# Early weight chunks and a diagonal-matrix mix for the first batch of a linear-attention, channel-mix and expert-attention kernel

## The chip, the cores and the metric

The kernel runs on one core of one Trainium2 chip. The metric is the device time of one execution in microseconds (us). A profile shows one execution; its span begins and ends a little inside that execution's own time.

## What is computed

Eight batches of 576 positions go through three blocks. The change touches the first two of them. The reference, cut to these:

```python
kv = np.einsum('bhsd,bhse->bhde', k, v)          # 8 heads of 64
out = np.einsum('bhsd,bhde->bhse', q, kv)
rms = np.sqrt(np.mean(out * out, axis=-1, keepdims=True) + 1e-06)
x = out / rms * g_norm                           # 512 columns in all
x_prev = x shifted by one position, zeros first
xk = mu_k * x + (1.0 - mu_k) * x_prev
xr = mu_r * x + (1.0 - mu_r) * x_prev
kk = np.maximum(xk @ w_k, 0.0)                   # w_k 512 x 1024
vv = kk * kk @ w_v                               # w_v 1024 x 512
x2 = vv / (1.0 + np.exp(-(xr @ w_r)))            # w_r 512 x 512
```

The weights w_r, w_k and w_v are given as float64. The third block, attention of four experts with a gate, reads x2 and stays as it is.

## The kernel before

**Shapes and loops.** Positions lie along the free axis, in two halves of 288 for each batch; features lie along the 128 partitions, in four slices. Each product of the second block is made as three single-pass products of a high and a low part (`mm3`, L60 to L64: wh times xh, wh times xl, wl times xh). `phase1` does the first two blocks batch by batch; `phase2` does the third.

**Weight conversion.** w_r, w_k and w_v are 20 chunks of 128 x 512 float64 numbers, 512 KB each: chunks 0 to 3 are w_r, 4 to 11 w_k, 12 to 19 w_v. `wload` (L134 to L138) asks for a chunk on ScalarE's queue, into one of three buffers `raw`. `wconv` (L167 to L191), at its call number i, finishes chunk i-1, asks for chunk i+2 and starts chunk i: ScalarE writes the magnitudes of the high words to `cvt` (L190), one of three buffers; the generator `words` (L140 to L158) then issues five VectorE steps (L146, L148, L150, L155, L157) and one ScalarE copy (L152); finally the low part is made by a full-precision product and two single-pass ones (L183 to L185) and a ScalarE copy (L186). Chunks 13, 15, 17 and 19 use two VectorE operations (L179, L180) instead of products. `wstep` issues one step of the chunk in work; it is called between the steps of a root.

**The front of a batch.** The generator `front(b)` multiplies keys with values of five position chunks (L229), asks for the next batch's first three key and value chunks, copies the sum to `kv` (L233), and then for each half: multiplies q (L251, `heads`), squares and copies (L256, L257), forms the means with products (L269), takes the reciprocal root on VectorE in 14 dependent steps (`rsqrt`, L276 to L291), spreads it with products (L299) and scales xT (L302). For batch 0 the halves go one after the other.

**The mix.** `mix(b, h, which)` makes the high and the low part of xr or xk of a half, slice by slice: ScalarE scales the shifted column block (L354), VectorE adds the scaled current one (L355), ScalarE rounds to the high part (L356), and the low part is a VectorE subtraction (L348), or, for xr of batch 0, a full-precision product with the identity, a single-pass product with its negative (L344, L345) and a ScalarE copy (L346). `acc`, the PSUM tile of all these products, has four buffers.

**Order.** First all loads are asked for (L415 to L427): weight chunks 0 to 2 on ScalarE's queue, keys, values and q of batch 0 on SyncE's, then the second batch's last two key and value chunks (L423, into tiles that are free until the first k product), and the small vectors. Then the front of batch 0 runs in seven steps with conversions between them as the list `TK` says (L453 to L457); then the xr mix of the first half with four more conversions; then the r products of the first half (L464) with the second batch's front and the second half's xr mix between them; then those of the second half with the first half's xk mix; then the main loop, with k products (L494), v products (L505) and, among the v products of the first half, the second half's xk mix (L508). This written order is not the order on the engines: the framework's scheduler orders each engine's instructions when the program is built, and sets one of a later line ahead of an earlier one where its own timeline has the engine free.

Of the kernel before, what the change touches and what calls it, by code (L numbers as in the profile page):

```python
# [8 lines left out]
F32 = mybir.dt.float32  # L9
F32R = mybir.dt.float32r  # L10
BF16 = mybir.dt.bfloat16
I32 = mybir.dt.int32
U32 = mybir.dt.uint32
AF = mybir.ActivationFunctionType
# [10 lines left out]
def tile_kernel(ctx: ExitStack, tc: tile.TileContext, qT, k, v, g2, mu_k, mu_r, w_r, w_k, w_v, w_qk, w_vg, w_o, out):  # L25
    nc = tc.nc
    P = 128
    B, S, DM = k.shape
# [3 lines left out]
    HS = S // 2  # L32
    KD = DM // P
# [9 lines left out]
    NF = len(FH)  # L43
# [5 lines left out]
    ident = const.tile([P, P], F32, name="ident")  # L49
    g_sb = const.tile([P, 1], F32, name="g_sb")  # L50
    muk = const.tile([P, KD], F32, name="muk")
    mur = const.tile([P, KD], F32, name="mur")
    nuk = const.tile([P, KD], F32, name="nuk")
    nur = const.tile([P, KD], F32, name="nur")
# [52 lines left out]
    def phase1():  # L107
        with ExitStack() as st1:
            w1 = st1.enter_context(tc.tile_pool(name="w1", bufs=1))
            sb = st1.enter_context(tc.tile_pool(name="sb1", bufs=2))  # L110
            ps = st1.enter_context(tc.tile_pool(name="ps1", bufs=1, space=PSUM))
# [13 lines left out]
            stg = stg_.enter_context(tc.tile_pool(name="stg", bufs=2, side="right"))  # L125
            CW = 512
# [3 lines left out]
            raws, cvs, ops = {}, {}, []  # L130

            VEC = (13, 15, 17, 19)

            def wload(i):  # L134
                if i < len(wts):
                    _, _, w, kt, c0 = wts[i]
                    raw = raws[i] = stg.tile([P, CW, 2], I32, name="raw", bufs=3)
                    nc.scalar.dma_start(raw.rearrange("p n t -> p (n t)"), w[kt * P:(kt + 1) * P, c0:c0 + CW].bitcast(I32))  # L138

            def words(i):  # L140
# [26 lines left out]
            def wconv():  # L167

                i = wat[0]
                wat[0] += 1  # L170
                if 0 < i <= len(wts):
                    for _ in ops.pop():
                        pass
                    wh, wl, _, kt, c0 = wts[i - 1]
                    x = cvs.pop(i - 1)
                    raws.pop(i - 1)
                    h, l = wh[:, kt, c0:c0 + CW], wl[:, kt, c0:c0 + CW]
                    if i - 1 in VEC:
                        nc.vector.tensor_sub(x, x, h.bitcast(F32))  # L179
                        nc.vector.tensor_add(l, x, l.bitcast(F32))  # L180
                    else:
                        acc = ps.tile([P, CW], F32, name="acc", bufs=4)
                        nc.tensor.matmul(acc, ident, x, start=True, stop=False)  # L183
                        nc.tensor.matmul(acc, idn, h, start=False, stop=False)
                        nc.tensor.matmul(acc, idn, l, start=False, stop=True)  # L185
                        nc.scalar.activation(l, acc, AF.Copy)  # L186
                    wload(i + 2)
                if i < len(wts):
                    t = cvs[i] = stg.tile([P, CW], F32, name="cvt", bufs=3)
                    nc.scalar.activation(t, raws[i][:, :, 1].bitcast(F32), AF.Abs)  # L190
                    ops.append(words(i))  # L191

# [2 lines left out]
            def load_kv(i, kv=None):  # L195
                b, c = divmod(i, NF)
                if b < B and i not in kvt:
                    t0, n = FH[c]
                    if kv is None:
                        kv = [(fr2[0] if c > 2 else fr).tile([P, DM], F32, name=name, bufs=2 if c > 2 else 3) for name in ("kt", "vt")]  # L200
                    kt, vt = kv
                    nc.sync.dma_start(kt[:n], k[b, t0:t0 + n, :])
                    nc.sync.dma_start(vt[:n], v[b, t0:t0 + n, :])
                    kvt[i] = (kt, vt)
# [12 lines left out]
            def front(b):  # L217
# [51 lines left out]
                                nc.tensor.matmul(sm[g:g + 32, :QS], sels[:, i, :], sqs[h, i // 2][:, i % 2, c * QS:(c + 1) * QS],  # L269
                                                 start=(i == 0), stop=(i == NP - 1), skip_group_check=True)  # L270

                def rsqrt(h0, h1):
                    g = slice(64 * h0, 64 * h1)
                    m, r, t, c = ms[g], y[g], nt[g], rb[g]

                    nc.vector.tensor_scalar(m, sm[g, :QS], -0.5, -0.5e-6, op0=ALU.mult, op1=ALU.add)  # L276
                    wstep()
                    nc.vector.tensor_scalar(t.bitcast(I32), m.bitcast(I32), 1, None, op0=ALU.logical_shift_right)
                    wstep()
                    nc.vector.tensor_scalar(r.bitcast(I32), t.bitcast(I32), -1.0, float(0x5F3759DF + 2 ** 30 - 2 ** 22), op0=ALU.mult, op1=ALU.add)  # L280
                    wstep()
                    for _ in range(3):
                        nc.vector.tensor_mul(t, r, r)
                        wstep()
                        nc.vector.tensor_mul(t, t, m)
                        wstep()
                        nc.vector.scalar_tensor_tensor(r, t, 1.5, r, op0=ALU.add, op1=ALU.mult)
                        wstep()

                    nc.vector.tensor_copy(c, r)  # L290
                    nc.vector.scalar_tensor_tensor(c, c.bitcast(F32), lom[g], r, op0=ALU.mult, op1=ALU.add)  # L291
# [12 lines left out]
                if b == 0:  # L304

                    for h in range(2):
                        for a in range(2):
                            heads(h, a)
                            yield
                        means(h)  # L310
                        rsqrt(h, h + 1)
                        yield
                        scaled(h)
                        yield
                    return
# [12 lines left out]
                    yield  # L328
                    yield

            mixed = {}

            def mix(b, h, which):
                mu, nu = (mur, nur) if which == "r" else (muk, nuk)
                xT = xTs[b]
                xh = sb.tile([P, KD, HS], F32R, name="xh", bufs=2)
                xl = sb.tile([P, KD, HS], F32R, name="xl", bufs=2)
                mixed[b, h, which] = (xh, xl)

                def low(p):  # L340
                    if b == 0 and which == "r":

                        acc = ps.tile([P, 512], F32, name="acc", bufs=4)
                        nc.tensor.matmul(acc[:, :HS], ident, xp, start=True, stop=False)  # L344
                        nc.tensor.matmul(acc[:, :HS], idn, xh[:, p, :], start=False, stop=True)  # L345
                        nc.scalar.activation(xl[:, p, :], acc[:, :HS], AF.Copy)  # L346
                    else:
                        nc.vector.tensor_sub(xl[:, p, :], xp, xh[:, p, :].bitcast(F32))  # L348

                for p in range(KD):  # L350
                    cur = xT[:, p, 1 + h * HS:1 + (h + 1) * HS]
                    prv = xT[:, p, h * HS:(h + 1) * HS]
                    x = sb.tile([P, HS], F32, name="xm", bufs=3)
                    nc.scalar.activation(x, prv, AF.Copy, scale=nu[:, p:p + 1])  # L354
                    nc.vector.scalar_tensor_tensor(x, cur, mu[:, p:p + 1], x, op0=ALU.mult, op1=ALU.add)  # L355
                    nc.scalar.activation(xh[:, p, :], x, AF.Copy)  # L356
                    if p > 0:
                        low(p - 1)
                    xp = x
                    yield  # L360
                low(KD - 1)
                yield
# [42 lines left out]
            def run(*gens):  # L405
                for g in gens:
                    if g is not None:
                        next(g, None)
# [3 lines left out]

            sk2 = [sb.tile([P, KF, HS], F32, name=name, bufs=1).rearrange("p k t -> p (k t)") for name in ("kh", "kl")]
            sq_ = sb.tile([P, KD, HS], F32, name="sg", bufs=2)
            for c in "w0 w1 w2 k0 k1 k2 k3 k4 q0 q1 q2 q3".split():  # L415
                i = int(c[1])
                if c[0] == "w":
                    wload(i)
                elif c[0] == "k":
                    load_kv(i, [sk[:, j * DM:(j + 1) * DM] for j in (2 * i - 6, 2 * i - 5)] if i > 2 else None)  # L420
                else:
                    load_q(i, sq_[:, :2, :] if i > 2 else None)
            for i in (3, 4):  # L423
                load_kv(NF + i, [t[:, (i - 3) * DM:(i - 2) * DM] for t in sk2])
            nc.sync.dma_start(g_sb, g2)
            nc.sync.dma_start(muk, mu_k)
            nc.sync.dma_start(mur, mu_r)  # L427
# [21 lines left out]
            def ticks(n):  # L449
                for _ in range(n):  # L450
                    wconv()

            TK = [1, 0, 1, 1, 0, 1, 1, 1, 1, 1, 1]  # L453
            wconv()
            for i in range(7):
                run(f0)
                ticks(TK[i])  # L457
            mr = mix(0, 0, "r")
            for i in range(4):
                run(mr, f0)  # L460
# [3 lines left out]
            for m in range(KD):  # L464
                r_group(0, 0, m)
                run(f1, mr)
                wconv()
            run(f1, mr)
            mk = mix(0, 0, "k")
            for m in range(KD):  # L470
                r_group(0, 1, m)
# [405 lines left out]
```

## Time and profile before

| | us |
|---|---|
| median of three runs | 1022.28 |
| the three runs | 1023.65, 1022.28, 1021.43 |
| the profiled execution, its own time | 1020.85 |
| its span | 1018.8 |
| TensorE busy in the span | 987.1 |
| VectorE busy | 546.8 |
| ScalarE busy | 500.2 |

In the rows, PE is TensorE's products, PEld its weight loads, DVE is VectorE, ACT ScalarE, POOL GpSimd, SP SyncE; ACTq and SPq are the queues of the latter two, in which transfers are started. L12 is line 12 of the kernel. A row names the tile written and the tiles read, the shape and type of each, and how often. A full-precision product appears as two records. Products are pipelined, and the lengths of neighbouring ones overlap; the distance of their starts tells what one costs.

### The profile page before, as it was taken

Reading aid. Unit: us, or ns where it says so; the run is one execution under the profiler, and the core shown is the slowest. Engines: PE = TensorE matmul, PEld = TensorE weight load, DVE = VectorE, ACT = ScalarE, POOL = GpSimd, SP = SyncE. Lnnn points to the kernel's source line nnn. Section 1 sums busy time; section 2 is a strip of 40 time slices with the busy share of each in tenths; the row PEclk is TensorE's granted clock in tenths of the full one; section 3 lists DMA queues with packets and bytes.
Section 4 is the critical chain, followed back from the end, with each engine's and each line's share of the span. In section 5 each row is a group of like instructions: output and inputs, shape, how many; then the busy total and the mean of one; then the engine's idle time right before and its main releaser. Section 6 shows DMA issues by size and latency. Waiting matters only on the chain.

```text
span 1018.8 us, 21026 instructions
## 1 busy us (share of the span) xinstructions
PE 987.1 (97%) x8168; PEld 899.7 (88%) x8168; DVE 546.8 (54%) x1572; ACT 500.2 (49%) x1326; POOL 248.5 (24%) x408
## 2 busy tenths in 40 slices
PE   6789999999999999999999999999999999999998
PEld 3358999999999999999999999988989898888986
DVE  4889625535535535445355531476575655656552
ACT  4677426434533553463364533456463645464544
POOL 0001212102201210220131113265161625334321
PEclk9789999999999999999999999999999999999999
DMA  9572213041050050050002201211120202020102
GB/s 324 171 231 64 67 60 106 24 112 53 25 151 27 10 164 24 1 165 24 24 2 71 60 5 43 69 48 31 65 71 24 94 1 94 18 77 27 48 12 82
DMA packets 42034, 70.56 MB, mean 69 GB/s; under 512 B 3792, under 2 KB 21712, under 8 KB 41936
## 3 DMA queue, kind: packets, MB, share of 16 engines
q1 hardware_dynamic: 30608, 49.31, 15.4%
q10 hardware_dynamic: 11328, 19.93, 6.3%
q8 instruction: 64, 1.05, 0.5%
q14 instruction: 34, 0.28, 0.1%
HBM read 50.34 MB, written 18.87 MB: 68 GB/s over the span
## 4 chain that ended last, share of the span: by engine, by line
PE 80%; DMA 7%; ACT 4%; POOL 3%; DVE 3%; issue 1%; ACTq 0%; SPq 0%; DVEq 0%; POOLq 0%
PE acc L62 22%; PE acc L64 21%; PE acc L63 21%; PE acc L725 3%; PE pt L698 3%; DMA x2in<-x2d 3%; PE s L649 2%; PE po L251 2%; POOL pr L678 2%; POOL x2l L535 2%; ACT pr L661 2%; PE acc L229 1%; PE acc L269 1%; ACT x2h L534 1%; PE po L299 1%
## 5 line engine op out<-in xcount | busy, mean ns | idle before, releaser
L388 POOL TENSOR_TENSOR ksq<-rl 128x288 f32<-128x288 f32 x128 | 92.8, 727 | 502.8 <-ACT rl L385 475.8
L62 PE MATMUL acc<-xh,wkh 128*128 128x288 f32 x512 | 153.2, 299 | 0.0
L64 PE MATMUL acc<-xh,wkl 128*128 128x288 f32 x512 | 151.6, 296 | 0.0
L64 PE MATMUL acc<-kh,wvl 128*128 128x288 f32 x512 | 151.1, 296 | 0.0
L62 PE MATMUL acc<-kh,wvh 128*128 128x288 f32 x512 | 149.4, 297 | 0.5 <-ACT kh L386 0.4
L63 PE MATMUL acc<-kl,wvh 128*128 128x288 f32 x512 | 149.6, 293 | 0.2 <-DVE kl L389 0.2
L63 PE MATMUL acc<-xl,wkh 128*128 128x288 f32 x512 | 149.4, 292 | 0.0
L661 ACT ACTIVATE pr<-pr,nm 128x256 f32<-128x256 f32 (+4 forms) x144 | 83.2, 580 | 66.5 <-DVE nm L615 65.6
L389 DVE TENSOR_TENSOR kl<-ksq,kh 128x288 fp32r<-128x288 f32 x128 | 64.4, 507 | 72.3 <-POOL ksq L388 70.6
L62 PEld LDWEIGHTS acc<-xh,wkh 128*128 128x128 f32 x512 | 96.2, 188 | 7.1 <-issue 5.3
L678 POOL TENSOR_SCALAR pr<-pr,rc,wg 128x512 f32<-128x512 f32 (+3 forms) x128 | 76.6, 613 | 99.3 <-DVE wg L608 53.9
L63 PEld LDWEIGHTS acc<-kl,wvh 128*128 128x128 f32 x512 | 97.3, 190 | 0.7 <-DVE kl L389 0.4
L63 PEld LDWEIGHTS acc<-xl,wkh 128*128 128x128 f32 x512 | 97.4, 190 | 0.1
L62 PEld LDWEIGHTS acc<-kh,wvh 128*128 128x128 f32 x512 | 95.3, 188 | 1.4 <-ACT kh L386 0.9
L64 PEld LDWEIGHTS acc<-kh,wvl 128*128 128x128 f32 x512 | 96.1, 188 | 0.0
L64 PEld LDWEIGHTS acc<-xh,wkl 128*128 128x128 f32 x512 | 96.0, 188 | 0.0
L374 ACT ACTIVATE sg<-acc 128x288 f32<-128x288 f32 x64 | 25.9, 408 | 142.6 <-PE acc L64 142.6
L348 DVE TENSOR_TENSOR xl<-xm,xh 128x288 fp32r<-128x288 f32 x120 | 54.4, 487 | 75.9 <-ACT xh L356 75.3
L401 DVE TENSOR_TENSOR sg<-acc,sg 128x288 f32<-128x288 f32 x64 | 29.2, 457 | 105.9 <-PE acc L64 105.1
L385 ACT ACTIVATE rl<-acc 128x288 f32<-128x288 f32 x128 | 52.1, 414 | 58.7 <-PE acc L64 58.3
L62 PE MATMUL acc<-x2h,wqh 128*128 128x256 f32 (+1 forms) x256 | 78.6, 308 | 0.0
L62 PE MATMUL acc<-xh,wrh 128*128 128x288 f32 x256 | 77.1, 302 | 1.1 <-ACT wvl L186 1.1
(166 smaller groups left out, 2437.3 us busy)
## 6 DMA issues: line engine op xcount, KB each, us to landing
x2d<-sg SPq DMA_DIRECT2D x16, 576.0 KB, 3.3
qt<-in_qT SPq DMA_DIRECT2D x31, 288.0 KB, 4.8
out<-ob SPq DMA_DIRECT2D x28, 288.0 KB, 2.1
kt<-in_k SPq DMA_DIRECT2D x24, 256.0 KB, 5.2
vt<-in_v SPq DMA_DIRECT2D x24, 256.0 KB, 5.7
x2in<-x2d ACTq DMA_DIRECT2D x8, 640.0 KB, 4.4
raw<-in_w_k ACTq DMA_DIRECT2D x8, 512.0 KB, 4.5
raw<-in_w_v ACTq DMA_DIRECT2D x8, 512.0 KB, 3.5
```

The lines of the kernel that those rows point to most:

```text
L62: nc.tensor.matmul(ps, wh(i), xh(i), start=(i == 0), stop=False)
L63: nc.tensor.matmul(ps, wh(i), xl(i), start=False, stop=False)
L64: nc.tensor.matmul(ps, wl(i), xh(i), start=False, stop=(i == n - 1))
L348: nc.vector.tensor_sub(xl[:, p, :], xp, xh[:, p, :].bitcast(F32))
L385: nc.scalar.activation(rl, acc, AF.Relu)
L388: nc.gpsimd.tensor_mul(sq, rl, rl)
L389: late.append(lambda: nc.vector.tensor_sub(kl[:, m, :], sq, kh[:, m, :].bitcast(F32)))
L401: nc.vector.tensor_mul(sg[:, m, :], acc, sg[:, m, :])
L661: nc.scalar.activation(pr[:, :L], pr[:, :L], AF.Exp, bias=nm, scale=-1.0, accum_out=sms[b, p, j][:, e2:e2 + 1])
L678: nc.gpsimd.tensor_scalar(pr[:, :L], pr[:, :L], rc[:, r:r + 1], wg, op0=ALU.mult, op1=ALU.mult)
L698: nc.tensor.transpose(pt[:, (i - i0) * P:(i - i0 + 1) * P], pr[:, k1 - P:k1], ident)
L725: nc.tensor.matmul(y[r * D:(r + 1) * D, a:w], vs[:, i, e * D:(e + 1) * D], pT[:, r, i, a:w], start=(i == 0), stop=(i == idx[-1]), skip_gro ...
```

## The change

Four edits to `phase1`; all else stays.

- **Loads.** Chunks 3 and 4 are asked for at the start too, into tiles `xh` and `xl` that the mixes use only later. Calls 1 to 3 of `wconv` then ask for chunks 5 to 7, calls 4 and 5 for none, and from call 6 on it is as before. The written order puts chunk 2 behind two pairs of keys and values, chunk 3 before the last pair, chunk 4 behind two q loads. The second batch's last two key and value chunks are asked for after the third step of the front instead of at the start.
- **Order.** `TK` has one more conversion in its second place. In the first root of batch 0 no conversion step is written between its steps.
- **Mix.** For batch 0 a slice is mixed by two full-precision products with diagonal matrices (mu and 1 - mu on the diagonal, made by ScalarE from the identity), the high part is copied out of PSUM, a single-pass product with the negative identity is added, and the low part is copied out. This serves all four mixes of batch 0.
- **Buffers.** `cvt` has two buffers instead of three; the diagonals (`dg`) have one.

```diff
-            def wload(i):
+            def wload(i, raw=None):
...
-                    raw = raws[i] = stg.tile([P, CW, 2], I32, name="raw", bufs=3)
+                    if raw is None:
+                        raw = stg.tile([P, CW, 2], I32, name="raw", bufs=3)
+                    raws[i] = raw
...
-                    wload(i + 2)
+
+                    if i - 1 < 3:
+                        wload(i + 4)
+                    elif i - 1 > 4:
+                        wload(i + 2)
                 if i < len(wts):
-                    t = cvs[i] = stg.tile([P, CW], F32, name="cvt", bufs=3)
+                    t = cvs[i] = stg.tile([P, CW], F32, name="cvt", bufs=2)
...
-                def rsqrt(h0, h1):
+                def rsqrt(h0, h1, wstep=wstep):
...
-                        rsqrt(h, h + 1)
+                        rsqrt(h, h + 1, *([lambda: None] if h == 0 else []))
...
+            def diag(which):
+                dg = dgs[which] = stg.tile([P, 2, KD, P], F32, name="dg", bufs=1)
+                for j, t in enumerate((mur, nur) if which == "r" else (muk, nuk)):
+                    for p in range(KD):
+                        nc.scalar.activation(dg[:, j, p, :], ident, AF.Copy, scale=t[:, p:p + 1])
...
+                if b == 0:
+
+                    dg = dgs[which]
+                    acc = None
+                    for p in range(KD + 1):
+                        if p > 0:
+                            nc.tensor.matmul(acc[:, :HS], idn, xh[:, p - 1, :], start=False, stop=True, skip_group_check=True)
+                            nc.scalar.activation(xl[:, p - 1, :], acc[:, :HS], AF.Copy)
+                        if p < KD:
+                            acc = ps.tile([P, 512], F32, name="acc", bufs=4)
+                            for j in range(2):
+                                nc.tensor.matmul(acc[:, :HS], dg[:, j, p, :], xT[:, p, 1 - j + h * HS:1 - j + (h + 1) * HS], start=(j == 0), stop=(j == 1))
+                            nc.scalar.activation(xh[:, p, :], acc[:, :HS], AF.Copy)
+                        yield
+                    return
...
-            for c in "w0 w1 w2 k0 k1 k2 k3 k4 q0 q1 q2 q3".split():
+            sw = [sb.tile([P, KD, HS], F32R, name=name, bufs=2).rearrange("p k t -> p (k t)")[:, :2 * CW].bitcast(I32).rearrange("p (n t) -> p n t", t=2) for name in ("xh", "xl")]
+            for c in "w0 w1 k0 k1 w2 k2 k3 w3 k4 q0 q1 w4 q2 q3".split():
                 i = int(c[1])
                 if c[0] == "w":
-                    wload(i)
+                    wload(i, sw[i - 3] if i > 2 else None)
...
-            for i in (3, 4):
-                load_kv(NF + i, [t[:, (i - 3) * DM:(i - 2) * DM] for t in sk2])
...
-            TK = [1, 0, 1, 1, 0, 1, 1, 1, 1, 1, 1]
+            TK = [1, 1, 1, 1, 0, 1, 1, 1, 1, 1, 1]
             wconv()
             for i in range(7):
                 run(f0)
+                if i == 2:
+                    for c in (3, 4):
+                        load_kv(NF + c, [t[:, (c - 3) * DM:(c - 2) * DM] for t in sk2])
                 ticks(TK[i])
+                if i == 4:
+                    diag("r")
             mr = mix(0, 0, "r")
...
             run(f1, mr)
+            diag("k")
             mk = mix(0, 0, "k")
```

## Rows read from the trace of the kernel before

**Rows 1.** The page's first part: busy time, share of the span and instructions of each engine.
```profile
PE 987.1 (97%) x8168; PEld 899.7 (88%) x8168; DVE 546.8 (54%) x1572; ACT 500.2 (49%) x1326; POOL 248.5 (24%) x408
```
**Rows 2.** Busy time by stretch: window, length, engines (records), TensorE's clock, transfers' share, GB/s.
```profile
0.00:20.70 20.70, 10.69 (x92) 5.99 (x92) 8.65 (x21) 6.58 (x12) 1.98 (x17) 1.00 0.94 318
20.70:35.20 14.50, 10.13 (x44) 4.43 (x44) 10.62 (x31) 7.27 (x14) 0.00 (x0) 0.76 0.87 289
35.20:68.30 33.10, 27.17 (x203) 16.61 (x203) 27.93 (x65) 24.83 (x51) 0.00 (x0) 0.81 0.57 185
68.30:89.80 21.50, 20.39 (x147) 15.80 (x146) 19.41 (x42) 18.62 (x44) 0.00 (x0) 0.98 0.41 125
89.80:104.10 14.30, 14.30 (x103) 13.64 (x102) 14.30 (x31) 9.45 (x23) 6.29 (x8) 1.00 0.11 39
```
**Rows 3.** Timeline of ScalarE and its queue: start, length, instruction, idle before it.
```profile
19.98 0.34 ACTq L138 DMA_DIRECT2D raw<-in_w_k  x1
20.36 0.38 ACT L233 ACTIVATE kv<-acc 128x256 f32<-128x256 f32 x1 [3.42 <-DMA kl<-in_v]
...
47.59 0.66 ACT L190 ACTIVATE cvt<-raw 128x512 f32<-128x512 f32 x1 [0.27 <-DMA raw<-in_w_k]
...
50.76 0.68 ACT L190 ACTIVATE cvt<-raw 128x512 f32<-128x512 f32 x1 [1.50 <-DMA raw<-in_w_k]
```
**Rows 4.** Timeline of VectorE, first root: first step, its one gap, last step.
```profile
24.77 0.30 DVE L276 TENSOR_SCALAR ms<-acc 64x144 f32<-64x144 f32 x1
...
27.73 0.43 DVE L146 TENSOR_SCALAR cvt<-cvt 128x512 f32<-128x512 f32 x1 [1.11 <-ACT cvt L190]
...
33.62 0.35 DVE L291 SCALAR_TENSOR_TENSOR rb<-rb,lom,y 64x144 fp32r<-64x144 f32 x1
```
**Rows 5.** Timeline of all engines, 36 to 62 us: the landmarks named in the text.
```profile
36.10 1.82 DVE L302 SCALAR_TENSOR_TENSOR xT<-xT,g_sb,po 128x288 f32<-128x288 f32 x4 [2.13 <-issue]
...
44.26 0.31 DVE L276 TENSOR_SCALAR ms<-acc 64x144 f32<-64x144 f32 x1 [1.22 <-PE acc L269]
...
49.47 0.29 PE L62 MATMUL acc<-xh,wrh 128*128 128x288 f32 x1
...
53.76 0.22 PE L229 MATMUL acc<-kl,kh 112*64 112x64 f32 x1
...
54.89 1.12 PE L183 MATMUL acc<-cvt,ident 128*128 128x512 f32 x2
...
60.06 0.67 PE L299 MATMUL po<-rb,selb 32*128 32x144 f32 x8 [1.98 <-DVE rb L291]
```
**Rows 6.** Timeline of TensorE at the full clock.
```profile
75.85 0.65 PE L344 MATMUL acc<-xm,ident 128*128 128x288 f32 x2
...
76.47 1.02 PE L183 MATMUL acc<-cvt,ident 128*128 128x512 f32 x2
...
77.80 0.65 PE L344 MATMUL acc<-xm,ident 128*128 128x288 f32 x2
...
89.88 0.30 PE L62 MATMUL acc<-xh,wkh 128*128 128x288 f32 x1
90.01 0.29 PE L63 MATMUL acc<-xl,wkh 128*128 128x288 f32 x1
```
**Rows 7.** Groups by line and form, first 89.8 us: busy, mean ns, idle before.
```profile
L354 ACT ACTIVATE xm<-xT,nur 128x288 f32<-128x288 f32 x8 | 4.0, 533 | 0.7 <-DVE xT L302 0.7
L355 DVE SCALAR_TENSOR_TENSOR xm<-xT,mur,xm 128x288 f32<-128x288 f32 x8 | 3.9, 513 | 1.0 <-ACT xm L354 1.0
...
L346 ACT ACTIVATE xl<-acc 128x288 fp32r<-128x288 f32 x8 | 3.3, 418 | 0.3 <-issue 0.3
...
L348 DVE TENSOR_TENSOR xl<-xm,xh 128x288 fp32r<-128x288 f32 x4 | 1.7, 450 | 0.0
...
L444 ACT ACTIVATE idn<-ident 128x128 fp32r<-128x128 f32 x1 | 0.3, 309 | 0.0
```
**Rows 8.** Transfers of the first 100 us: issue, KB, us to landing.
```profile
kl<-in_v SPq DMA_DIRECT2D x1, 160.0 KB, 8.0
```

More of the change, by code (lines that the diff above doesn't have):

```diff
@@ L329, in front @@
                     yield
-            mixed = {}
+            mixed, dgs = {}, {}
+            def diag(which):
[3 more added lines that the diff above has]
+                        nc.scalar.activation(dg[:, j, p, :], ident, AF.Copy, scale=t[:, p:p + 1])
             def mix(b, h, which):
@@ L338, in mix @@
                 mixed[b, h, which] = (xh, xl)
-                def low(p):
[L341 to L348, printed above, removed]
+                if b == 0:
[12 more added lines that the diff above has]
+                    return
+                def low(p):
+                    nc.vector.tensor_sub(xl[:, p, :], xp, xh[:, p, :].bitcast(F32))
                 for p in range(KD):
```

## The prediction

> **What bounds the kernel now.** The page's first part comes first: TensorE is busy 97% of the span [rows 1]. The stretches of the first 104 us show where the rest is. I count as lost what a stretch leaves over after TensorE's busy time multiplied by its granted clock: 20.7 - 10.69 x 1.00 = 10.0 us, 14.5 - 10.13 x 0.76 = 6.8, 33.1 - 27.17 x 0.81 = 11.1, 21.5 - 20.39 x 0.98 = 1.5, and nothing in the last: 29.4 us [rows 2]. The first k product starts at 89.88 [rows 6], and from there TensorE is full. So **the end is TensorE's work plus the time it loses before 90 us**; a change pays what it adds to the one and gains what it takes from the other. VectorE is busy 14.30 of 14.3 us in the last stretch and 19.41 of 21.5 before it, but TensorE loses little there: what VectorE is spared after 68 us buys almost nothing [rows 2].
>
> What loses the 29.4 us is read from the order on each engine. The copy of kv, behind which all of the first half stands, ran at 20.36 us, because a weight load sat in ScalarE's queue until 19.98 and waited for a load of values to land; ScalarE idled 3.42 us for it [rows 3]. The first root began at 24.77 and its last step at 33.62, 9.2 us to its end, with ten conversion steps of two chunks (the first at 27.73) and a gap of 1.11 us among its fourteen [rows 4]. From its scaling (36.10) to the first r product (49.47) pass 13.4 us; the second root runs from 44.26 to the product that reads it, 60.06 [rows 5]. Inside it ScalarE waited 1.50 us for a weight chunk [rows 3].
>
> **What the change costs on TensorE.** A full-precision product of 288 columns and its correction took 76.47 - 75.85 = 0.62 us at the full clock, a single-pass product 90.01 - 89.88 = 0.13, so the full one is 0.49 [rows 6]. The mix of one 128-row slice becomes two full products and one correction, 1.11 us; four mixes of four slices are 16 x 1.11 = 17.8 us. Gone are the eight full products and eight corrections of the two r mixes, 8 x 0.62 = 5.0. **TensorE's work grows by 12.8 us**, and by the accounting above all of it is paid; the last mix, 4.4 us, stands among the v products after 104 us, where nothing can cover it.
>
> **What it moves off the other engines.** VectorE loses 16 multiply-adds of 0.51 us and the 8 subtractions of the k mixes of 0.45, 11.8 us [rows 7]. ScalarE loses 16 scalings of 0.53 (8.5 us) and gains 8 copies of the low part of 0.42 (3.3) and 16 diagonals; the nearest row for one is the 128x128 copy of 0.31, so 5.0 [rows 7]. That is even, taken as nothing. The first eight diagonals stand beside the first root, where ScalarE is busy half of the time; the other eight (2.5 us) fall where it is busy 18.62 of 21.5 us, and could be felt if a copy stood behind them [rows 2].
>
> **What it recovers** of the 29.4, stretch by stretch [rows 2]:
> - *To 20.7 us.* Chunks 3 and 4 are asked for early. Chunk 3 can be converted while TensorE waits for keys, 1.3 us of its work (three products from 76.47 to 77.80 [rows 6]). ScalarE's 3.42 us before the kv copy may go, 2.7 of them after the last key product; but chunk 5's load takes the place of chunk 3's in ScalarE's queue: it waits for chunk 0's buffer, and behind it stand the magnitudes of the next chunks and the kv copy. Against it, chunk 3's 512 KB go ahead of the last keys, at 318 GB/s 1.6 us. Ends -1.6 and 4.0; I take 2.5, nearer to the upper end, since the queue wait is the longer of the two.
> - *To 35.2.* The root's own fourteen steps, the first 0.30 and the last 0.35, are by estimate 4.2 us [rows 4] of 9.2. Ends 0 and 5.0. I take 3.5: the gap of 1.11 goes and chunks 3 and 4 lie behind VectorE, but steps of a chunk written later stood inside this root too, so some will again.
> - *To 68.3.* From scaling to the first r product I get 1.8 us of scaling, four slices of two ScalarE copies (4 x 0.84), and one slice's latency of 3.1 at 1.2 GHz (two products of 0.98, two copies, a correction), 8.3 us by estimate from [rows 5 to 7], against 13.4. The second root keeps its interleaving; what goes is the mix among its steps and, as chunks 5 to 7 are asked for two conversions earlier, waits such as the 1.50. Chunk 8 onwards is asked for as before. Ends 0 and 11.1; I take 8.5, the 5.1 just found and some of the second root.
> - *To 89.8.* TensorE is without work 1.1 us. Ends 0 and 1.5; I take 1.2.
>
> Sum: 2.5 + 3.5 + 8.5 + 1.2 = 15.7 recovered, 12.8 paid: **-2.9 us**. The ends, all together, are -8.8 and +14.4.
>
> The Trainium skill (DMA: Bandwidth & Descriptors, Issuing engines are not separate DMA queues) says that transfers started by different engines run on the same 16 engines and interleave, so that another issuing engine saves little more than issue time. By it the early chunks only displace keys, the first term is -1.6, and the sum is +1.2. The transfer engines, 94% busy in the first 20.7 us, support it [rows 2]; the held kv copy is a wait of ScalarE's queue, of which it does not speak.
>
> **Edits with no price.** The loads of the second batch's last keys and values go behind that batch's first three pairs on SyncE's queue. The slowest took 8.0 us to land [rows 8]; their first reader runs at 53.76 [rows 5], and asked for at 27 us they are there by 35: free while that lead of 18 us stands. The q loads behind them start four issues later and serve products after 60 us. The small mu loads move up. One conversion earlier in the written order moves no work off any engine. The mixes hold a PSUM buffer over two ScalarE copies instead of one: between nothing and 16 x 0.42 = 6.7 us, taken as nothing, since four buffers stand in turn and a slice comes only between groups.
>
> **The rivals.** *The roots stay filled (slower).* Ten conversion steps of two chunks stood in the first root although the code writes only one chunk's there [rows 4]; with two more chunks landed there is more to put in. Then the second stretch gives 0, the third 5.0, the first 1.0, the last 0: 6.0 recovered, +6.8, 1029.1. It decides as soon as less than 10.8 is recovered. Against it: it needs the filling to be as dense while VectorE has 11.8 us less to do. The Trainium skill (Perfetto Trace Analysis, Identifying the Most-Contended Engine) points the same way: improve the engine with the highest occupancy first; this change loads it. TensorE's 97% agrees that it is that engine.
> *VectorE paced the front.* If its 11.8 us come through almost whole, all stretches go near their ends: 21 recovered, -8.2, 1014.1. For it: VectorE is busy 27.93 of 33.1 us in the third stretch; against it: 8.65 of 20.7 and 10.62 of 14.5 in the first two [rows 2].
> *The two cancel*, within 2 us: 1022.3.
> *Two conversion buffers pace the chunks (slower).* A chunk held its buffer from its magnitudes (47.59 [rows 3]) to the end of its first product (54.89 and 0.56 [rows 5]), 7.9 us; with two buffers that is a chunk every 3.9 us, where the next one came after 3.2 (50.76). Over the eight chunks of w_v that is 5.6 us, and the first v product waits for the last of them: 1025.
>
> **How the numbers follow.** The profiled execution took 1020.85 us by its own time, 2.05 around its span, and the runs' median is 1022.28, 1.43 above it; -2.9 gives 1017.95 beside the profile and 1019.4 beside the median. Under 0.2%, 2 us, a measurement of this kernel cannot be told from no change. Chances: the forecast (2 to 6 us faster) 0.28, VectorE as pacer 0.20, cancelling 0.20, filled roots 0.24, two buffers 0.08. So faster 0.48, same 0.20, slower 0.32. The likeliest case's own range is 1016 to 1020; cases of both signs hold the chance, so the range goes from 1012, which leaves out the best part of the pacer case, to 1029, which takes in most of the filled roots.
>
> **What would show it.** Right: the kv copy before 20 us; the first root in under 6 us; the first r product before 45; the first k product some 7 us before 89.88, although 8.4 of the added 12.8 us stand ahead of it (all but the last mix); the granted clock near 1.00 from 35 us. Wrong: conversion steps inside the first root as densely as now, a kv copy behind a weight load, magnitudes waiting for a conversion buffer, or a first k product later than 85.5 us, which leaves no room for the last mix.

## The result, and the profile after

The changed kernel takes 1033.95 us, the median of four runs (1033.38 to 1035.8), the kernel before 1021.86 on the same chip: ratio 1.0126 [1.0109, 1.0143]. **It is slower by 12 us**, outside the predicted range. The profiled execution took 1033.38 us, its span 1031.6, 12.8 more than before. Lines of the changed kernel stand up to 20 further down: the weight load is L140, the magnitudes L196, the full-precision product of a conversion L185, the kv copy L239, the diagonals L343, the mix L358 to L364.

The page's first part after [rows 1]:
```profile
PE 997.5 (97%) x8224; PEld 909.9 (88%) x8224; DVE 536.5 (52%) x1548; ACT 501.3 (49%) x1334; POOL 246.2 (24%) x408
```
VectorE is relieved by 10.3 us, ScalarE is even, TensorE has the added work. The same stretches as in [rows 2]:
```profile
0.00:20.70 20.70, 9.37 (x48) 4.78 (x50) 9.42 (x24) 6.39 (x10) 1.87 (x16) 0.92 0.95 329
20.70:35.20 14.50, 11.11 (x94) 6.14 (x90) 9.98 (x26) 12.18 (x26) 0.11 (x1) 0.85 0.92 305
35.20:68.30 33.10, 24.27 (x183) 16.05 (x183) 22.89 (x56) 14.85 (x30) 0.00 (x0) 0.81 0.46 152
68.30:89.80 21.50, 21.50 (x130) 15.35 (x129) 14.41 (x28) 18.66 (x43) 0.00 (x0) 0.99 0.47 153
89.80:104.10 14.30, 14.30 (x111) 12.17 (x110) 12.99 (x32) 8.18 (x18) 0.00 (x0) 1.00 0.12 38
```
By the prediction's formula (length less busy time times granted clock) TensorE loses 12.1, 5.1, 13.4, 0.2 and 0: **30.8 us, where the kernel before lost 29.4** and the forecast left 13.7. Nothing was recovered. The first k product starts at 98.4 (before 89.88), the first v product at 114.0 (104.1).

**The start.** ScalarE and its queue after [rows 3]:
```profile
15.55 0.34 ACTq L140 DMA_DIRECT2D raw<-in_w_k  x1
16.01 0.66 ACT L196 ACTIVATE cvt<-raw 128x512 f32<-128x512 f32 x1 [5.07 <-DMA xT<-in_k]
...
24.49 0.38 ACT L239 ACTIVATE kv<-acc 128x256 f32<-128x256 f32 x1 [0.55 <-PE acc L235]
...
28.30 1.28 ACT L343 ACTIVATE dg<-ident,mur 128x128 f32<-128x128 f32 x4
29.47 1.28 ACT L343 ACTIVATE dg<-ident,nur 128x128 f32<-128x128 f32 x4
30.64 0.65 ACT L262 ACTIVATE sq<-po 128x576 f32<-128x576 f32 x1
```
A weight load (15.55, chunk 5) sat in the queue until keys had landed, by the row that names what ended the wait, and with the magnitudes behind it ScalarE idled for 5.07 us. TensorE's rows show what follows:
```profile
18.37 2.07 PE L185 MATMUL acc<-cvt,ident 128*128 128x512 f32 x2 [3.30 <-DVE cvt L152]
20.38 1.12 PE L235 MATMUL acc<-vt,kt 128*64 128x64 f32 x16
21.43 0.80 PE L186 MATMUL acc<-wrh,idn 128*128 128x512 f32 x1
22.02 0.63 PE L187 MATMUL acc<-wrl,idn 128*128 128x512 f32 x1
22.58 1.86 PE L235 MATMUL acc<-xT 112*64 112x64 f32 x32
```
The late magnitudes make the conversion's product late, and the products of keys and values (L235) stand behind it in TensorE's order. So the kv copy runs at 24.49 instead of 20.36. Then eight diagonals (1.17 us for four, by the distance of their starts) stand ahead of the second squares, and the first root starts at 32.15 instead of 24.77. The diagonals are the smaller part of that: in `e5_nomix` below, which has none, the root starts at 30.60.

**The first root and the mix.** VectorE [rows 4]: the root's first step, a conversion step of each of the two chunks in it, and its last step:
```profile
32.15 0.30 DVE L282 TENSOR_SCALAR ms<-acc 64x144 f32<-64x144 f32 x1 [0.91 <-PE acc L275]
32.40 0.43 DVE L148 TENSOR_SCALAR cvt<-cvt 128x512 f32<-128x512 f32 x1
...
34.19 0.41 DVE L148 TENSOR_SCALAR cvt<-cvt 128x512 f32<-128x512 f32 x1
...
39.80 0.36 DVE L297 SCALAR_TENSOR_TENSOR rb<-rb,lom,y 64x144 fp32r<-64x144 f32 x1
```
Ten conversion steps stand in it, as before, though none is written there: 8.0 us to its end, against 9.2. TensorE waits for it; its products in time order [rows 5], then its windows (TensorE's busy time is the second number, its clock the third from the end):
```profile
40.31 1.13 PE L305 MATMUL po<-rb,selb 32*128 32x144 f32 x8 [6.15 <-DVE rb L297]
41.68 2.29 PE L363 MATMUL acc<-xT,dg 128*128 128x288 f32 x4 [0.25 <-DVE xT L308]
46.28 1.24 PE L363 MATMUL acc<-xT,dg 128*128 128x288 f32 x4
51.31 1.24 PE L363 MATMUL acc<-xT,dg 128*128 128x288 f32 x4
53.71 1.13 PE L363 MATMUL acc<-xT,dg 128*128 128x288 f32 x4
56.15 0.29 PE L62 MATMUL acc<-xh,wrh 128*128 128x288 f32 x1
```
```profile
36.00:40.00 4.00, 0.00 (x0) 0.00 (x0) 3.83 (x13) 0.63 (x1) 0.00 (x0) 0.50 0.52 163
40.00:44.00 4.00, 3.44 (x13) 2.70 (x14) 1.95 (x5) 0.00 (x0) 0.00 (x0) 0.50 0.30 103
...
41.11:56.15 15.04, 14.79 (x72) 8.41 (x70) 8.88 (x21) 8.70 (x18) 0.00 (x0) 0.88 0.19 61
```
TensorE has no product from 36 to 40 us; in the 4 us behind that the granted clock is still 0.50, that is 1.2 GHz, and the first slice's four records take 2.29 us instead of 1.24. And from the scaling (41.11) to the first r product (56.15) pass 15.0 us, in which **TensorE is busy 14.79**: it paces the mix itself. Before, the same distance was 13.37 us, with TensorE busy 11.59 and VectorE 11.86:
```profile
36.10:49.47 13.37, 11.59 (x59) 5.96 (x57) 11.86 (x28) 11.20 (x24) 0.00 (x0) 0.79 0.36 112
```

### The profile page after: what moved, and what is told of

Its sections match the earlier page's. It is cut to its first block, busy times and chain, and to the rows that moved or that the text cites. A ratio compares the mean times of both kernels' runs of the same rounds, so it can differ in the third digit from the quotient of the medians.

```text
span 1031.6 us, 21112 instructions
## 1 busy us (share of the span) xinstructions
PE 997.5 (97%) x8224; PEld 909.9 (88%) x8224; DVE 536.5 (52%) x1548; ACT 501.3 (49%) x1334; POOL 246.2 (24%) x408
## 4 chain that ended last, share of the span: by engine, by line
PE 86%; DMA 4%; ACT 3%; POOL 3%; DVE 3%; issue 1%; ACTq 0%; DVEq 0%; POOLq 0%
PE acc L62 23%; PE acc L64 22%; PE acc L63 22%; PE pt L724 3%; PE acc L751 3%; PE s L675 2%; DMA x2in<-x2d 2%; PE po L257 2%; PE acc L235 2%; ACT pr L687 2%; POOL x2l L561 2%; PE acc L363 2%; POOL pr L704 1%; PE acc L185 1%; PE acc L275 1%; PE po L305 1%
## 5 line engine op out<-in xcount | busy, mean ns | idle before, releaser
L369 DVE TENSOR_TENSOR xl<-xm,xh 128x288 fp32r<-128x288 f32 x112 | 50.8, 490 | 75.9 <-ACT xh L377 75.3
L422 DVE TENSOR_TENSOR sg<-acc,sg 128x288 f32<-128x288 f32 x64 | 29.3, 457 | 114.0 <-PE acc L64 113.3
```

The lines of the kernel that those rows point to most:

```text
L422: nc.vector.tensor_mul(sg[:, m, :], acc, sg[:, m, :])
```

## The experiments

All ratios are to the kernel before on the same chip, with a 95% interval. Edits are shown against the kernel before, or as a part of the diff above. "Lost" is TensorE's lost time to 104.1 us by the formula above (before: 29.4).

**The mix with its buffers, alone.** `e1_mix` is the kernel before with the mix and the buffers edit.

> The kernel before with the diagonal mix alone (and the two conversion buffers that make room for the diagonals). Theory 1, the products are paid: TensorE's added 12.8 us come through whole, 1021.9 + 12.8 = 1034.7, and the first root starts within 1 us of 24.8. Theory 2, the early loads cost half: by the two profiles the first root starts 7.4 us later in the changed kernel, so here, with the old loads, half of the 12 us is missing: 1026 to 1029.

1030.16 us, 1.009 [1.0077, 1.0103], lost 27.5: between the two theories. So of the 12.8 us of products some 3 to 4 come back. `e5_nomix` is the rest of the change: the loads, order and buffers edits, with the old mix.

> The changed kernel with the old mix: early loads, root without written conversion steps, one conversion earlier, two conversion buffers. Theory 1: no different from the kernel before, 1020 to 1024, though the first root starts late. Theory 2: 5 to 7 us slower, 1027 to 1029, first root near 32 us.

1024.04, 1.0036 [1.0022, 1.005]: the time of theory 1, nearly, with the first root late (30.60) as both had it. So that lateness costs at most 3.7 us. What the changed kernel has beyond it is the mix: 1.0126 - 1.0036, 9.2 us. So its 12.8 us of span are not the 12.8 of products, though the two numbers agree: some 9 come with the mix and 3.7 with the rest. (`e1_mix` and `e5_nomix` both have the two buffers.)

**The loads edit, by two queues.** `e2_loads` is that edit alone. `e11_loads_sp` asks for the weight chunks on SyncE's queue as well:

```diff
-                    nc.scalar.dma_start(raw.rearrange("p n t -> p (n t)"), w[kt * P:(kt + 1) * P, c0:c0 + CW].bitcast(I32))
+                    nc.sync.dma_start(raw.rearrange("p n t -> p (n t)"), w[kt * P:(kt + 1) * P, c0:c0 + CW].bitcast(I32))
```

> The kernel before with the loads edit alone, three conversion buffers. Theory 1: 1020 to 1024. Theory 2: 1026 to 1029, with the kv copy near 24.5 us as in the changed kernel, since ScalarE's queue holds the sixth chunk's load until a key load has landed.

> The loads edit alone, with the weight chunks asked for on SyncE's queue instead of ScalarE's. If ScalarE's queue made the kv copy late (24.1 us with the edit, 20.4 without), the copy comes back to 20 to 22 us and the first root to 25 to 28. If the chunks' bytes ahead of the keys did, the copy stays at 23 to 25. By time 1019 to 1024 either way.

1024.28, 1.0024 [1.0013, 1.0036], and 1019.49, 0.9988 [0.9976, 1.0]: 3.7 us apart. ScalarE's timeline up to the kv copy, first from `e2_loads`:
```profile
15.43 0.33 ACTq L140 DMA_DIRECT2D raw<-in_w_k  x1
15.89 0.66 ACT L195 ACTIVATE cvt<-xh 128x512 f32<-128x512 f32 x1 [5.09 <-DMA xT<-in_v]
...
24.06 0.39 ACT L238 ACTIVATE kv<-acc 128x256 f32<-128x256 f32 x1
```
and from `e11_loads_sp`:
```profile
15.98 0.67 ACT L195 ACTIVATE cvt<-xh 128x512 f32<-128x512 f32 x1 [1.87 <-DMA xh<-in_w_r]
...
18.86 0.37 ACT L238 ACTIVATE kv<-acc 128x256 f32<-128x256 f32 x1
```
Without loads in its queue ScalarE does not stand behind the keys, and the kv copy runs 5.2 us earlier. The order in which transfers start changes with the queue too: SyncE asks for chunks 3 and 4 at 7.35 and 12.04, ScalarE at 2.14 and 4.48. But that does not make the difference, for the last values land no earlier: at 16.9 in `e11_loads_sp` (asked for at 8.70, 8.2 to landing), at 16.6 in `e2_loads` (10.52 and 6.1). The early chunks themselves gain some 1.2 us, with an interval that reaches no change.

**The order edit, alone.** `e3_order`:

> The kernel before with the order edit alone: one more conversion in the second place of TK, and no conversion step written inside the first root of batch 0. Theory (the written order is only a proposal, the scheduler fills the root with steps of chunks written elsewhere): the first root still holds steps of conversions and is within 1 us of its 9.2 us; the time is within 2 us of before (ratio 0.998 to 1.002). Rival (the root does come in one piece): no conversion step between its fourteen, it ends some 3.5 us earlier, and the time is 2 to 4 us under before (0.996 to 0.998).

1022.49, 1.0018 [1.0007, 1.0029]. Its first root (7.9 us), from the second step on:
```profile
27.61 0.23 DVE L278 TENSOR_SCALAR nt<-ms 64x144 int32<-64x144 int32 x1
27.76 0.41 DVE L146 TENSOR_SCALAR cvt<-cvt 128x512 f32<-128x512 f32 x1
28.10 0.22 DVE L280 TENSOR_SCALAR y<-nt 64x144 int32<-64x144 int32 x1
28.24 0.41 DVE L148 TENSOR_SCALAR cvt<-cvt 128x512 int32<-128x512 int32 x1
```
Ten steps of conversions, again: the scheduler takes them from chunks written elsewhere.

**The mixes, one by one.** `f1_rmix3` has only the xr mixes by products (diagonals in the tiles of the second batch's keys and values, three conversion buffers); `f5_three3` adds the first xk mix; `f2_lastold` is `e1_mix` with the last xk mix back on VectorE:
```diff
-                if b == 0:
+                if b == 0 and (h == 0 or which == "r"):
```

> The kernel before with the diagonal mix for the two r mixes only, three conversion buffers. 3.9 us of products are added, half of them in the stretch where TensorE waits. Theory A: 1023 to 1026. Theory B: 1019 to 1022.

> The kernel before with the diagonal mix for both r mixes and the first k mix, the last k mix as before, and three conversion buffers (the diagonals lie in a tile that is free until the k products). Theory A, products are paid wherever TensorE is full: 8.4 of the 12.8 us are added here, of which at most 2 are covered: 1027 to 1030. Theory B, the two conversion buffers and the last mix were the cost of the mix alone (5.5 and 4.4 against 8.9 measured): 1020 to 1023.

> The run with the mix alone, its last k mix (among the v products) back on VectorE; two conversion buffers. Both theories: the last mix's 4.4 us of products stood in a full stretch and go, 1030.2 - 4.4 = 1025.8. If less than 2 us go, products that stand between full stretches are not what costs.

1020.05, 0.9998 [0.9987, 1.0008]; 1023.57, 1.003 [1.0019, 1.0041]; 1026.88, 1.006 [1.0044, 1.0076]. Theory B holds for the first; the second lies between A and B. The xr mixes' 3.9 us (8 x (1.11 - 0.62)) cost nothing: `f1_rmix3` lost 25.2, which is 4.2 less, nearly all of it here:
```profile
35.20:68.30 33.10, 29.79 (x205) 19.06 (x205) 25.40 (x59) 21.20 (x43) 0.00 (x0) 0.89 0.52 171
```
TensorE is busy longer than in [rows 2], and at 0.89 instead of 0.81. Each xk mix, priced at 4.4, shows with some 3 us (3.3 and 3.1 by the ratios).

**The two buffers.** `e4_cvt2` is the buffers edit alone. `h1_mix_cvt3` is `e1_mix`, `h2_after_cvt3` the changed kernel, both with three buffers. To make room, the diagonals of the fourth slice are left out: its products use those of the third, so its values are not the reference's; TensorE's work is the same, and ScalarE makes 12 diagonals instead of 16.
```diff
-  dg = dgs[which] = stg.tile([P, 2, KD, P], F32, name="dg", bufs=1)
+  dg = dgs[which] = stg.tile([P, 2, KD - 1, P], F32, name="dg", bufs=1)
...
-  t = cvs[i] = stg.tile([P, CW], F32, name="cvt", bufs=2)
+  t = cvs[i] = stg.tile([P, CW], F32, name="cvt", bufs=3)
```

> The kernel before with two conversion buffers instead of three. Both theories: 1020 to 1024. Theory 3, the buffers pace the chunks: 1024 to 1028, the last magnitudes well after 92.5 us.

> The kernel before with all four mixes of batch 0 by products, and three conversion buffers. The tile of diagonals holds three slices of four; the fourth slice uses the third's diagonals, so its values are not the reference's, and ScalarE makes 12 diagonals instead of 16; TensorE's work is that of the full mix. Theory (two buffers cost some 3 us beside the products): 3 us under the same kernel with two buffers (1.009), that is 1.005 to 1.007. Rival (with the products the buffers are no limit, and the 9 us are the products'): 1.008 to 1.010.

> The changed kernel with three conversion buffers (the same smaller tile of diagonals: the fourth slice uses the third's, so its values are not the reference's; 12 diagonals instead of 16). Theory (two buffers cost some 3 us): 1.009 to 1.0105 against 1.0126. Rival (no limit here): 1.0115 to 1.0135.

1026.85, 1.0063 [1.0043, 1.0083]; 1026.98, 1.0059 [1.0045, 1.0074]; 1033.34, 1.013 [1.0111, 1.0148]. Alone, the edit costs 6 us, beside the mix 3, **in the changed kernel nothing**, each to some 2 us. Alone it does what the prediction's last rival says: the last magnitudes run at 99.78 instead of 92.47, and TensorE loses 7.1 us from 68.3 to 104.1, where it lost 1.5. The changed kernel loses 0.2 us there, so a third buffer has no gap to close. ScalarE's waits for a conversion buffer to 115 us (total, times, longest), of `e4_cvt2`, the changed kernel and `h2_after_cvt3`:
```profile
ACT cvt L190 <- PE acc L183: 3.7, 3, 1.6
```
```profile
ACT cvt L196 <- PE acc L185: 2.9, 5, 1.1
```
```profile
ACT cvt L196 <- PE acc L185: 2.6, 3, 1.4
```
The kernel before has no such wait. The third buffer leaves the last two nearly alike: with it the magnitudes still stand behind such a product.

**Down from the changed kernel.** `g2_after_sp` is the changed kernel with its weight loads on SyncE's queue; `h3_after_sp_cvt3` has three buffers as well; `h4_after_sp3_lastold` also has the last xk mix on VectorE (and all 16 diagonals, laid as in `f1_rmix3`); `g4_best` also the first xk mix; `g1_rmix_sp` is `g4_best` without the order edit.

> The changed kernel whole, with the weight chunks asked for on SyncE's queue instead of ScalarE's. Theory (the parts add, and the held queue of ScalarE is one of them): the kv copy runs before 21 us instead of 24.5, and the time is 3 to 4 us under the changed kernel, that is 8 to 9 over before (ratio 1.008 to 1.009). Rival (the front's lateness is absorbed by conversions running ahead, so that only the products and the two buffers cost): the kv copy is as early, but the time stays at 12 over before (1.0115 to 1.013).

> The changed kernel with its weight loads asked for on SyncE's queue and with three conversion buffers (the same smaller tile of diagonals, the fourth slice's values not the reference's). Theory (the two costs add): 1.0035 to 1.0055 against 1.0073 with two buffers. Rival (no limit here): 1.0065 to 1.008.

> The changed kernel with its weight loads asked for on SyncE's queue, three conversion buffers (the diagonals lie in the tiles of the second batch's keys and values, all 16 of them) and the last xk mix back on VectorE. Theory (all costs add: the queue 5, the buffers 3, the last mix 3 off the changed kernel's 12): within 2 us of before, 0.999 to 1.002. Rival (what is left of the added products shows, 8.4 us less what the xr mixes hide): 4 us over before or more, from 1.004.

> The run before this one (loads on SyncE's queue, xr mixes by products, three conversion buffers) with the order edit as well. Theory (the order moves nothing): the same within 1 us as without the order edit, 0.998 to 0.999. Rival (with the xr mix off VectorE and more chunks landed, the uninterrupted root shows): 3 or more under before, 0.997 or less.

> The kernel before with the loads edit asked for on SyncE's queue and the two xr mixes of batch 0 by products (three conversion buffers, xk mixes as before, both roots as before). Theory (the parts add: 0 for the xr mixes, -1.2 for the loads): 1 to 2 us under before, ratio 0.998 to 0.999. Rival (with the front earlier, the stretch in which TensorE waits and in which the xr products hid is gone, and their 3.9 us show): 2 to 4 over before, 1.002 to 1.004.

| kernel | us | ratio | step down, us | lost, us |
|---|---|---|---|---|
| changed | 1033.95 | 1.0126 [1.0109, 1.0143] | | 30.8 |
| g2_after_sp | 1027.78 | 1.0073 [1.0061, 1.0085] | 5.4 | 25.0 |
| h3_after_sp_cvt3 | 1028.92 | 1.0079 [1.0057, 1.01] | -0.6 | 22.8 |
| h4_after_sp3_lastold | 1025.65 | 1.0046 [1.0029, 1.0063] | 3.4 | 26.9 |
| g4_best | 1019.82 | 0.9997 [0.9985, 1.0009] | 5.0 | 23.9 |
| g1_rmix_sp | 1021.81 | 1.0014 [1.0005, 1.0024] | | 29.3 |

A step is the difference of two ratios times 1021 us, and is good to some 2 to 3 us. **Taken down in this order, the 12 us are the two xk mixes (8.4 by these steps, 8.9 by price) and the held queue (5.4)**; the rest is within 1 us of nothing. (Added to the kernel before, the xk mixes showed with some 3 us each.) With the queue freed the kv copy of `g2_after_sp` runs at 20.25. The buffers' 3 us, forecast for `h2_after_cvt3` and `h3_after_sp_cvt3`, did not come. Three more forecasts fell here: `h4_after_sp3_lastold` was to come out even and is 4.7 us over, since the buffers gave nothing and the first xk mix cost all of its price; `g1_rmix_sp`, whose parts alone had given 0 and -1.2, is 1.4 over; and `g4_best`, with the order edit, which alone cost 1.8, is even and met neither of its forecasts. Parts add here to some 3 us and no better. That the scheduler sets the whole front anew with each edit would do this; it is not shown. No version beats the kernel before by more than a measurement can tell.

In `h4_after_sp3_lastold` the first root did come nearly in one piece. Its steps from the twelfth on:
```profile
31.07 0.30 DVE L292 SCALAR_TENSOR_TENSOR y<-nt,y 64x144 f32<-64x144 f32 x1
31.71 0.43 DVE L148 TENSOR_SCALAR cvt<-cvt 128x512 f32<-128x512 f32 x1 [0.34 <-ACT cvt L195]
32.05 0.22 DVE L295 CAST rb<-y 64x144 fp32r<-64x144 f32 x1
32.20 0.41 DVE L150 TENSOR_SCALAR cvt<-cvt 128x512 int32<-128x512 int32 x1
32.53 0.35 DVE L296 SCALAR_TENSOR_TENSOR rb<-rb,lom,y 64x144 fp32r<-64x144 f32 x1
```
It took 5.3 us (from 27.54), 2.4 less than the one of `g4_best` (7.7), and ended 1.2 later than that one, but the first r product came at 54.6, 5.6 later. The steps of two chunks that were not done within the root stand right behind it on VectorE, and among the scalings, which end 1.8 later (37.40, against 35.56); the other 3.8 us were not followed.

## Why the prediction was wrong

**The accounting held.** Products added less time recovered, that is lost time before less lost time after, gives -0.3 for `f1_rmix3` (3.9 - 4.2; its span changed by -0.3), -1.6 for `g4_best` (measured -1.6) and 8.4 for `g2_after_sp` (12.8 - 4.4; measured 7.8). For the change it gives 12.8 + 1.4 = 14.2, measured 12.8. In the other runs it comes within some 1.5 us of the span. The exception is `e4_cvt2`, 3.7 against 8.6: there the profiled execution (1030.23 us, mean granted clock 0.986) lay 3.4 us over the median of its six; the fastest, 1024.28, had 0.993. The products' price, 12.8, stands to about 1 us.

**What failed is "What it recovers": 15.7 us by the forecast, -1.4 in the changed kernel, 4.4 with the queue freed.** Stretch by stretch:

- *To 20.7 us*, taken at +2.5, came out at -2.1. The text named the load of chunk 5 that takes chunk 3's place in ScalarE's queue, with the magnitudes and the kv copy behind it, and then priced it at nothing. It let it wait for chunk 0's buffer only; the last step that reads that buffer (L159, from 10.19) was done at 10.9, and the load went at 15.55. This queue costs 5.4 us in all. `g2_after_sp`, without it, gives -0.2: there the early chunks delay the values, which the text allowed 1.6 us for. The last ones land at 18.7 (before 14.0), and the kv copy runs behind them. With a third buffer as well the 2.5 do come in two runs (2.4 in `g4_best`, 2.7 in `h3_after_sp_cvt3`) and not in two others (0.6 in `g1_rmix_sp`, -0.2 in `h4_after_sp3_lastold`).
- *To 35.2*, taken at 3.5 for a root in one piece: the lost time fell by 1.7, but since everything came 7 us later, other work lies in this window. The root kept its ten steps, and `e3_order` shows that the edit alone does not remove them. Where the steps did go, nothing was gained.
- *To 68.3*, taken at 8.5, came out at -2.3 (+3.4 in `g2_after_sp`). 5.8 of the missing 10.8 go with the held queue: the wait for the root, to 40.31, now lies in this window. The other 5.1 are a mistake of their own. The estimate of 8.3 us from the scaling to the first r product (measured: 15.0) was the latency of one slice after another. It left out that TensorE has its conversions and the second half's q products in the same stretch, and starts them at the low clock, which the estimate had for one slice only. TensorE is busy 14.79 of 15.04 us there. The product mix takes work off VectorE, which had been close to full there, and puts it on the engine that was nearly as full.
- *To 89.8*, taken at 1.2: 1.3, with other work in this window too.

**The rivals.** *The roots stay filled* had the sign, and its fact is in the trace; its price (6.8 over) is about half of the loss; in `h4_after_sp3_lastold` the filling went and the time stayed 4.7 over. *VectorE paced the front* falls as a forecast, 21 us recovered: the most of any run is 6.6. It is not without ground: `f1_rmix3` takes 5.1 us off VectorE and recovers 4.2, which its 3.9 us of products use up. The same edit takes scalings off ScalarE, and no run separates the two. *Two conversion buffers* is true of the kernel before (6 us) and not of the changed one (`h2_after_cvt3`: no gain to some 2 us). *The two cancel* is true of the xr mixes alone. No rival had the held queue; the list of signs had it ("a kv copy behind a weight load").

**The two rules weighed.** By the rule of the Trainium skill (DMA: Bandwidth & Descriptors, Issuing engines are not separate DMA queues) the issuing engine matters little, as all transfers share the same engines. `e2_loads` and `e11_loads_sp` differ by the issuing engine, and by 3.7 us: not for the transfers, whose last values land within 0.3 us of each other, but for the computing that stands behind a load which waits in its engine's queue. The other rule of the Trainium skill (Perfetto Trace Analysis, Identifying the Most-Contended Engine), to improve the engine with the highest occupancy first, speaks against a change that loads it. The two xk mixes bear it out: they load TensorE, and 8.4 of 8.9 us show. The two xr mixes do not: their 3.9 us go to the same engine where it loses time, and cost nothing.

**Open.** Of the 12.8 us of span, 8.5 are there at the first k product, 9.9 at the first v product, 11.6 at the last v product (650.5 against 638.9). The last 1.2 come in the third block, which was not touched, and were not followed. Why a weight load waits for keys that go to other tiles was not tried; that its wait ends with them is in the rows.

## What to carry to other kernels

Before a transfer is moved to an earlier place, look at what its issue waits for and which computing stands behind it in the same engine's queue; on an engine that only starts transfers no computing stands behind a load that waits, on one that computes it does. The stretch in which two engines were nearly full gave nothing when work went from one to the other: count the busy time of the receiving engine there, not the latency of the chain. And an amount of work that equals the loss is no proof: here the products' 12.8 us matched the span's 12.8, while 3.9 of them were hidden and a held queue of 5.4 us took their place.

## What was not expected of the hardware

The price of one buffer less depends on what surrounds it: 6 us on the kernel before, 3 beside the mix, none in the changed kernel, each to some 2 us. And idleness costs twice: after the 4 us in which TensorE waited for the root, the granted clock was 0.50 for the next 4 us too, while it was busy 3.44 of them, and the same four records took 2.29 us instead of 1.24.
